# Two load queues shared out anew, a split last output tile, and a new table of due times in an attention and MLP kernel

## The chip, the cores and the metric

The kernel runs on one core of a Trainium2 chip. The metric is device time in microseconds (us) of one execution. A profile gives, beside the time, the span from the first to the last instruction of the program and what each engine did in it: PE (TensorE, matmuls), PEld (its weight loads), DVE (VectorE), ACT (ScalarE), POOL (GpSimd) and SP (SyncE, which here only issues DMAs).

## The reference

A linear attention over 8 batches and 8 heads of 576 positions of 64 features, and an MLP (512 to 2048 to 512, ELU between) over the 4608 tokens that come out of it.

```python
def phi(x):
    proj = np.einsum('bhsd,md->bhsm', x, omega)
    h = proj - np.sum(x * x, axis=-1, keepdims=True) / 2.0
    return np.exp(h - np.max(h, axis=-1, keepdims=True)) / np.sqrt(m)
q_p, k_p = phi(q * scale), phi(k * scale)          # m = 128, scale = 64 ** -0.25
kv = np.einsum('bhsm,bhsd->bhmd', k_p, v)
z = np.sum(k_p, axis=2)
num = np.einsum('bhsm,bhmd->bhsd', q_p, kv)
den = np.einsum('bhsm,bhm->bhs', q_p, z)[..., None] + 1e-06
x = (num / den).transpose(0, 2, 1, 3).reshape(4608, 512)
h = x @ w_in
g = np.where(h > 0.0, h, np.exp(np.minimum(h, 0.0)) - 1.0)
out = g @ w_out
```

w_in and w_out come as 64-bit floats.

## The kernel before, in words

The 64 heads are worked on as 32 pairs (two heads of 64 features fill 128 partitions), and the tokens as 9 blocks of 512. For each pair the keys are loaded (`xk`), squared, projected on the features (`ppk`, PE), their row minima taken (`mnk`, DVE) and exponentials made (`hk`, ACT, nine instructions of 128 columns); with the values `v` they give `pkv` (PE) and from it `kvf` and `z`. The queries go the same way (`xq`, `ppq`, `mnq`, `hq`); `pz` (PE) spreads `z`, DVE sums the denominators with it, `pt` (PE) turns the normalised queries, ACT copies them (`qh`), and `pn` (PE) makes the pair's attention output, which ACT and DVE write as a rounded part `xh` and a rest `xl`. Pairs 0 to 7 take this way with 32-bit matmuls (lines 551, 656, 844, 901); pairs 8 to 31 first split their inputs into two parts (`tk`, `tq`, line 419) and use line 601.

Layer 1 of the MLP makes, for a block and one of 16 slices of 128 hidden features, `ph` out of 12 matmuls of 512 columns (lines 1049 to 1051); ACT and DVE make the ELU out of it (`e`), which is split in `g`; layer 2 adds 12 matmuls to four accumulators `acc` (line 1094). The first two blocks go through the first eight slices, then through the others; in these first passes the weights are made out of 64-bit words (`raw_w`, `u_w`, `w1c`, `w2h`, `w2l`, lines 977 to 1010, five DVE instructions and an ACT one or two for each) and layer 1's are stored (`w1s`) and later loaded again into one of two buffers `w1c` (line 1030).

The order of all this is not the order of the code. Each step is an entry with an engine (or several that could do it), an expected duration, a due time and its buffers; a planner (`Plan.order`) plays them through before anything is built, starts on each free engine the ready entry that is due first, and the instructions are written out in the order found. Each engine then takes its own in that order and waits for the others by semaphores. The due times come from constants at the top (`MLP0`, `SEG`, `DUE_K`, `OFF1`, ...), `ALT` says how much an engine other than the first is held back for a kind of step, `STICK` how long PE keeps to a kind of matmul, `DMA_LAT` what a load is expected to take. An entry with `port=True` on DVE is not planned beside one on POOL, and POOL's next gets a wait for it.

At the start, pair 0's keys come in three pieces (positions 0 to 255 and 256 to 511 of both heads and the last 64) from SP, its queries in two from ACT's queue. At the end, each of the last block's four output tiles `o` of 128 tokens is copied by ACT and stored by SP.

Of the kernel before, what the change touches and what calls it, by code (L numbers as in the profile page):

```python
# [19 lines left out]
P = 128  # L20
# [23 lines left out]
NNAT = dict(k=8, q=8)  # L44


MLP0 = 32.36
SEG = [6.77, 5.04, 5.8, 7.72]
STEP = 6.67
STEP_ATT = 6.98  # L50

LAG = 3.0


PAIR0 = 12.06
DUE_LOAD, DUE_K, DUE_KV, DUE_Q = 63.96, 29.35, 20.2, 25.97
LOAD2, K2, KV2, Q2 = -116.39, 43.14, 31.66, 29.71
TAIL = 12.1
TAIL2 = 7.09
HEAD = 12.38  # L60


CONV1 = 9.62
CONV_STEP = -0.88
CONV2 = -8.25

EARLY = 12.91
CONV3 = 54.99


CROSS = False
# [1 line left out]
SPLIT = (0, 8, 16)  # L73
NHALF = 2

DUE_Z = 16.24


TURNED = 8
EARLIER = 10.63  # L80
QB = 32
NQB = P // QB
NTURN = 4
# [31 lines left out]
class Plan:  # L115
# [13 lines left out]
    SHARED = ("DVE", "POOL")  # L129

    FREE = dict(PE=1100.0, ACT=730.0, DVE=1600.0, POOL=1300.0, SP=700.0)
    DMA_LAT, DMA_RATE = 1500.0, 360.0

    def __init__(self):
        self.tasks, self.writer, self.readers, self.lands, self.behind = [], {}, {}, {}, {}
# [181 lines left out]


YIELD = 2e6
STICK = 1.25  # L320
SWITCH = 90.0
ENGINES = dict(DVE=mybir.EngineType.DVE, POOL=mybir.EngineType.Pool)


OFFP = [2.21, -0.6, 8.06, 9.4, -0.61, 1.49, 6.23, 2.21, 1.88, 6.13, -0.21, -0.78]
OFF1 = [6.25, -6.74, 0.99, -6.97, 4.74, 10.22, -12.88, -2.8, 6.03, 3.53, 4.6, 7.5, -11.77, 3.17, 9.25, 6.43]
OFF2 = [-6.65, 6.52, -4.52, -15.46, -12.1, -12.39, -1.42, -19.38, 26.89, 12.78, 21.89, 7.05, -2.21, 4.79, 12.27, -9.31]
DUE_V = 19.0


ALT = {'out': 46, 'conv_hi': 56, 'conv_sub': 10, 'g_lo0': -34, 'sq0': 5, 'sq1': -9, 'sq2': 1, 'norm0': 17, 'norm1': 112, 'norm2': 95, 'y_hi0': 95, 'y_hi1': 29, 'y_lo0': 40, 'y_lo1': 10, 'turn0': 73, 'turn1': 48, 'x_hi0': 36, 'x_hi1': 35, 'kv0': -6, 'kv1': 17, 'g_hi0': 65, 'g_hi1': 19, 'g_hi2': 19, 'g_lo1': -48, 'g_lo2': 34}


def other(kind, *engs):
# [3 lines left out]
def mm(n, m=1):  # L338

    return m * (n / 2.4 + 13.3)  # L340
# [15 lines left out]
def performer_elu_kernel(  # L356
# [110 lines left out]
    def load_pair(i, due):  # L467
        s = st.setdefault(i, {})

        def dma(dst, src, nbytes, *writes, early=False):  # L470
            nonlocal due
            if early:
                op("ACT", 600, -900 + due, lambda: nc.scalar.dma_start(dst(), src), (), writes, nbytes)
            else:
                op("SP", 590, due, lambda: nc.sync.dma_start(dst(), src), (), writes, nbytes)
            due += 0.01

        for nm, nat, mixed in (("k", k, kx), ("q", q, qx)):
# [21 lines left out]
    def project(i, nm, due):  # L500
# [15 lines left out]
        if native(i, nm):  # L516
# [25 lines left out]
            for g in range(3):  # L542
# [10 lines left out]
                def view(p=p):  # L553
                    return p().rearrange("p (j x) -> p j x", j=4)

                op("PE", 872 if g < 2 else 218, d, mms, [*([(x, g, 2)] if apart else [(x, a, 2) for a in range(2)]), "of"], (p,), full=1)
# [34 lines left out]
        for c in range(5):  # L591
# [11 lines left out]
            def view(p=p):  # L603
                return p().rearrange("p (a x) -> p a x", a=2)

            op("PE", mm(256, n) + 20, d, mms, [(y, a, z) for a in range(2) for z in "hl"] + ["oh", "om"], (p, (h, "slot", c)))
            def rest(c=c, n=n, p2=p2, view=view):
                for a in range(n):
                    j = 2 * c + a
# [339 lines left out]
    def from_f64(src, hi, lo, nm, due, key):  # L949
# [22 lines left out]
        def tail():  # L972
# [63 lines left out]
    def layer1(F, due):  # L1036
# [15 lines left out]

        for c in range(NC):
            reads = [(z, k) for k in ring(blk) if k[1] == c for z in ("xh", "xl")]
            op("PE", 688, due + 0.5 * c, lambda c=c: mms(c), [*reads, (w, "h"), (w, "l")], (p,))
# [23 lines left out]
    def layer2(F, due):  # L1079
# [19 lines left out]
            runs = [((tt,), (0, 1, 2)) for tt in range(NTT)]  # L1099
        else:  # L1100
            runs = [((2 * h, 2 * h + 1), (0, 1)) for h in range(2)] + [((2 * h, 2 * h + 1), (2,)) for h in range(2)]
        for e, (tts, which) in enumerate(runs):
            d = due + 0.65 * e
            op(
                "PE", 230 * len(tts) * len(which), d, lambda tts=tts, which=which: mms(tts, which),
                [*((g, passes[n][0]) for n in which), *(("w2", f, passes[n][2]) for n in which)], [now[tt] for tt in tts],
            )
            if not last:
# [147 lines left out]
```

## Time and profile before

| | us |
|---|---|
| median of 3 runs (lowest to highest) | 996.37 (995.45 to 998.47) |
| the profiled execution: its own time | 996.64 |
| the profiled execution: span | 994.8 |
| busy in the span: PE, ACT, DVE, POOL | 985.8, 654.4, 570.3, 475.8 |

The profiled execution is one like the others: 0.27 us above the median. A matmul's end is modelled in the profile, so a PE that shows as busy may hold short stalls; its starts are as recorded. Idle time of an engine other than the one that bounds the kernel costs nothing by itself.

### The profile page before, as it was taken

The numbers are of one execution on the slowest core, as the hardware profiler recorded it, in microseconds if no ns is written. First come the engines' busy times: TensorE is split into PE (matmuls) and PEld (weight loads), VectorE is DVE, ScalarE is ACT, GpSimd is POOL, SyncE is SP. The second block draws the span as 40 slices with busy tenths as digits, with TensorE's granted clock in tenths as the row PEclk, the third lists the DMA queues.
The fourth block names the chain that finished last, engine by engine and source line by source line (L and its number), as shares of the span: only waits on it lengthen the run. The fifth ranks groups of instructions, "written<-read, shape, count | busy, mean of one in ns | idle before, by whom it ended". The sixth has DMA issues, their size and how long they took to land.

```text
span 994.8 us, 17293 instructions
## 1 busy us (share of the span) xinstructions
PE 985.8 (99%) x5232; PEld 807.1 (81%) x5232; DVE 570.3 (57%) x2283; ACT 654.4 (66%) x1730; POOL 475.8 (48%) x438
## 2 busy tenths in 40 slices
PE   9999999999999999999999999999999999999998
PEld 9887788887788787887788778878788778888886
DVE  7999999679666555555555545555555421212121
ACT  7997657998877768776777578776877322223222
POOL 4555202576356656664657556665665322222222
PEclk9999999999999999999999999999999999999999
DMA  8666785468685555655575646555563333324231
GB/s 223 180 200 232 241 281 193 164 226 308 201 280 183 192 187 176 220 170 163 156 236 178 203 158 229 182 197 186 173 210 111 122 119 129 106 85 148 85 106 63
DMA packets 66716, 179.12 MB, mean 180 GB/s; under 512 B 9472, under 2 KB 22208, under 8 KB 66624
## 3 DMA queue, kind: packets, MB, share of 16 engines
q1 hardware_dynamic: 66256, 177.70, 54.5%
q8 instruction: 42, 0.69, 0.3%
q14 instruction: 50, 0.41, 0.1%
q10 hardware_dynamic: 368, 0.33, 0.1%
HBM read 143.92 MB, written 34.08 MB: 179 GB/s over the span
## 4 chain that ended last, share of the span: by engine, by line
PE 89%; DVE 5%; ACT 4%; DMA 1%; issue 1%; SPq 0%; ACTq 0%
PE acc L1094 37%; PE ph L1049 13%; PE ph L1051 12%; PE ph L1050 12%; PE ppk L601 2%; PE ppq L601 2%; PE pn L737 2%; PE ppk L551 1%; PE ppq L551 1%; DVE u_w L1000 1%; PE pkv L656 1%; DVE junk L821 1%; DMA w1c<-w1s 1%; PE pz L800 1%; ACT p2k L610 1%
## 5 line engine op out<-in xcount | busy, mean ns | idle before, releaser
L1094 PE MATMUL acc<-w2h,g 128*128 128x512 f32 x1152 | 392.2, 393 | 0.0
L419 POOL TENSOR_TENSOR g<-e,g 128x512 fp32r<-128x512 f32 x128 | 166.4, 1300 | 275.1 <-DVE g L416 200.4
L1094 PEld LDWEIGHTS acc<-w2h,g 128*128 128x128 f32 x1152 | 214.1, 188 | 40.9 <-issue 0.2
L1049 PE MATMUL ph<-xh,w1c 128*128 128x512 f32 x576 | 229.1, 398 | 0.6 <-DMA w1c<-w1s 0.4
L1058 ACT ACTIVATE e<-ph 128x512 f32<-128x512 f32 x144 | 85.6, 595 | 217.3 <-PE ph L1051 215.6
L1094 PE MATMUL acc<-w2l,g 128*128 128x512 f32 x576 | 227.7, 395 | 0.0
L1051 PE MATMUL ph<-xh,w1c 128*128 128x512 f32 x576 | 226.3, 393 | 0.0
L1050 PE MATMUL ph<-xl,w1c 128*128 128x512 f32 x576 | 225.9, 392 | 0.0
L416 DVE CAST g<-e 128x512 fp32r<-128x512 f32 x128 | 58.8, 460 | 188.6 <-PE acc L1094 183.2
L1062 DVE SCALAR_TENSOR_TENSOR e<-e,ph 128x512 f32<-128x512 f32 x144 | 98.7, 685 | 56.2 <-ACT e L1059 52.3
L1049 PEld LDWEIGHTS ph<-xh,w1c 128*128 128x128 f32 x576 | 108.3, 188 | 26.4 <-PE pn L901 1.5
L1051 PEld LDWEIGHTS ph<-xh,w1c 128*128 128x128 f32 x576 | 108.3, 188 | 24.3
L1094 PEld LDWEIGHTS acc<-w2l,g 128*128 128x128 f32 x576 | 108.4, 188 | 21.9 <-issue 0.9
L1050 PEld LDWEIGHTS ph<-xl,w1c 128*128 128x128 f32 x576 | 108.4, 188 | 19.7
L419 POOL TENSOR_TENSOR hq<-hq,den 128x512 f32<-128x512 f32 (+1 forms) x96 | 79.2, 838 | 62.6 <-DVE den L830 39.4
L419 POOL TENSOR_TENSOR tk<-xk,tk 64x576 fp32r<-64x576 f32 x48 | 70.4, 1467 | 78.7 <-ACT tk L414 64.8
L419 POOL TENSOR_TENSOR tq<-xq,tq 64x576 fp32r<-64x576 f32 x48 | 69.0, 1437 | 58.4 <-ACT tq L414 29.8
L1059 ACT ACTIVATE e<-e 128x512 f32<-128x512 f32 x144 | 91.8, 638 | 1.9
L619 DVE CUSTOM_DVE_ANT_0 hq<-ppq,p2q 128x128 f32<-128x128 f32 x216 | 53.8, 287 | 55.4 <-ACT p2q L610 48.1
L610 ACT ACTIVATE p2k<-ppk,sqk 128x128 f32<-128x128 f32 x216 | 66.4, 370 | 24.1 <-PE ppk L601 16.7
L610 ACT ACTIVATE p2q<-ppq,sqq 128x128 f32<-128x128 f32 x216 | 67.6, 379 | 21.0 <-PE ppq L601 19.9
L821 DVE CUSTOM_DVE_ANT_0 junk<-hq,pz 128x128 f32<-128x128 f32 (+1 forms) x320 | 73.9, 281 | 8.1 <-PE pz L800 7.3
(172 smaller groups left out, 1340.9 us busy)
## 6 DMA issues: line engine op xcount, KB each, us to landing
w1c<-w1s SPq DMA_DIRECT2D x128, 512.0 KB, 3.5
raw_w<-in_w_dram SPq DMA_DIRECT2D x32, 512.0 KB, 4.3
xk<-in_kx_dram SPq DMA_DIRECT2D x24, 576.0 KB, 4.5
xq<-in_qx_dram SPq DMA_DIRECT2D x24, 576.0 KB, 4.9
turned<-tb SPq DMA_DIRECT2D x24, 576.0 KB, 3.4
qh<-turned SPq DMA_DIRECT2D x96, 144.0 KB, 4.9
v<-in_v_dram SPq DMA_DIRECT2D x32, 325.0 KB, 4.3
out_dram<-o SPq DMA_DIRECT2D x36, 256.0 KB, 3.6
```

Source lines behind the costliest of these rows:

```text
L416: nc.vector.tensor_copy(dst, src)
L419: (nc.vector if e == "DVE" else nc.gpsimd).tensor_tensor(*args)
L610: nc.scalar.activation(p2()[:, a], view()[:, a, M:], AF.Identity, bias=sq()[:, j:j + 1], scale=1.0)
L619: nc.vector.tensor_tensor_reduce(out=h()[:, j, :], in0=view()[:, a, 0:M], in1=p2()[:, a, :], scale=1.0, scalar=HIGHEST, op0=ALU.add, op1=A ...
L821: nc.vector.tensor_tensor_reduce(out=junk()[r], in0=h()[r, j, :], in1=pz()[r, a * P:(a + 1) * P], scale=1.0, scalar=EPS, op0=ALU.mult, op1 ...
L1049: nc.tensor.matmul(ph(), wh, xh[:, c, o:o + TB], start=(c == 0), stop=False)
L1050: nc.tensor.matmul(ph(), wh, xl[:, c, o:o + TB], start=False, stop=False)
L1051: nc.tensor.matmul(ph(), wl, xh[:, c, o:o + TB], start=False, stop=(c == NC - 1))
L1058: op("ACT", act(TB, True), due, lambda: nc.scalar.activation(e(), ph(), AF.Relu, scale=-1.0), (p,), (e,))
L1059: op("ACT", act(TB), due + 0.2, lambda: nc.scalar.activation(e(), e(), AF.Exp, scale=-1.0), (e,), (e,))
L1062: lambda: nc.vector.scalar_tensor_tensor(e(), e(), -1.0, ph(), ALU.add, ALU.max), (p, e), (e,),
L1094: nc.tensor.matmul(now[tt](), g()[:, a, ts], w(), start=(first and n == 0), stop=(last and n == 2))
```

## The change

1. **Pair 0's loads.** Keys piece 1 and 2 and the queries' last piece go over SP's queue; the keys' last piece and the queries' big piece over ACT's.
2. **The last output tile.** The last matmul of 512 columns becomes two of 256; the first half of the tile is copied by ACT and stored by SP, the second copied by DVE and stored from ACT's queue.
3. **The table.** All due times, offsets and `ALT` values are new, as are a few expected durations; one more of the five DVE instructions of the weights' conversion (line 1000) is marked `port=True`.

```diff
-MLP0 = 32.36
+MLP0 = 39.956
...
-ALT = {'out': 46, ... 'sq2': 1, ... 'y_lo0': 40, 'y_lo1': 10, ...}
+ALT = {'out': 86, ... 'sq2': 49, ... 'y_lo0': 46, 'y_lo1': 0, ...}
...
-                    dma(dst, nat[i][:, :, s0:s0 + n], 2 * P * max(n, 2 * D) * 4, (t, key), early=i == 0 and nm == "q")
+                    dma(dst, nat[i][:, :, s0:s0 + n], 3 * P * max(n, 2 * D) * 2, (t, key), early=i == 0 and (key == 1) == (nm == "k"))
...
-            "DVE", dve(512), due - 5,
+            "DVE", 645, due - 5,
...
-            (u, (raw, 0)), (u,),
+            (u, (raw, 0)), (u,), port=True,
...
+            op("PE", 460, d, most, reads, (a,))
+            for k in range(2):
+                c = slice(k * DM // 2, (k + 1) * DM // 2)
...
+                op("PE", 117, d + 0.1 * k, half, [*reads, a], ((a, k),))
+                op(
+                    *(("ACT", act(DM // 2, True)), ("DVE", dve(DM // 2)))[k], d + 0.3 * k,
+                    lambda c=c, k=k: copy(("ACT", "DVE")[k], o()[:, c], a()[:, c]), ((a, k),), ((o, k),),
+                )
+                q = (nc.sync, nc.scalar)[k]
+                op(
+                    ("SP", "ACT")[k], 590, d + 1, lambda c=c, q=q: q.dma_start(out[r:r + P, c], o()[:, c]), ((o, k),), (),
+                    P * DM * 2,
+                )
```

`early` sends a load over ACT's queue; `key` is 0, 3 and 1 for the keys' three pieces and 0 and 1 for the queries' two.

**ACT's first instructions** (`xk_96` are pair 0's keys, `xq` its queries), before:

```order
L422 DMA of<-in_omT_dram 64x128
L473 DMA xq_109<-in_q_dram 64x2x512
L473 DMA xq_109<-in_q_dram 64x2x64
L1159 ACT_TABLE_LOAD
L530 ACTIVATE xk_96<-xk_96 64x2x256 x2
```

and now:

```order
L422 DMA of<-in_omT_dram 64x128
L473 DMA xk_96<-in_k_dram 64x2x64
L473 DMA xq_110<-in_q_dram 64x2x512
L1191 ACT_TABLE_LOAD
L530 ACTIVATE xk_96<-xk_96 64x2x256 x2
```

The queries' big piece goes out second instead of first, behind the keys' small one.

**ACT before the last exponential of pair 7's keys** (`hk_1124`, with `hq_1193` the same pair's queries and `tk`, `u_w`, `w1c` work for later steps), before:

```order
L414 COPY z_1191<-pkv_1114 128x2
L511 ACTIVATE hq_1193<-ppq_0_1130,mnq_1171 128x128 x4
L414 COPY qh_1137<-pt_2_1162 128x2x64
L414 CAST tk_1116<-xk_1024 64x576
L414 CAST w2h<-u_w_1_1073 128x512
L982 ACTIVATE u_w_4_1219<-raw_w_4_1154 128x512
L414 CAST w1c_1233<-u_w_6_1169 128x512
L511 ACTIVATE hk_1124<-ppk_2_1157,mnk_1107 128x128
```

and now (`hk_1203` are pair 7's keys; `qh_1250` is pair 6's, `e_1259` and `e_1197` belong to layer 1):

```order
L1059 ACTIVATE e_1197<-e_1197 128x512
L414 CAST w2h<-u_w_4_1059 128x512
L982 ACTIVATE u_w_6_1234<-raw_w_6_1122 128x512
L414 CAST tk_1242<-xk_873 64x576
L414 COPY qh_1250<-pt_0_1236 128x2x256
L1058 ACTIVATE e_1259<-ph_1208 128x512
L414 COPY qh_1250<-pt_1_1244 128x2x256
L1059 ACTIVATE e_1259<-e_1259 128x512
L511 ACTIVATE hk_1203<-ppk_1_1183,mnk_1189 128x128 x4
L511 ACTIVATE hk_1203<-ppk_2_1195,mnk_1189 128x128
```

More of pair 6's copies and of layer 1 stands ahead of pair 7's keys. Counted from the start of the queue to that instruction, ACT now has 7 more squares of queries (line 530; 10 instead of 3), 1 more of keys and 1 fewer of the later pairs' (line 570), 2 more copies `qh` of 512 columns, 2 more instructions on `e`, 1 more on `u_w`, 2 more casts `xh`, 4 fewer exponentials `hq` and 1 fewer cast `tk`. On PE, the first matmul that needs it (`pkv` of pair 7) has 4 fewer matmuls of layer 2, 9 fewer projections of queries and 9 more turning matmuls `pt` ahead of it.

**The last instructions of DVE and ACT**, with the semaphores that each waits for, now (`o_end` is the last tile; before, DVE had nothing there and ACT copied all 512 columns):

```order
L416 CAST g_11043<-e_11012 128x512 [waits DVE_49,PE_49,Pool_49]
L416 COPY o_end<-acc_0_3_10616 128x256 [waits Activation_49]
...
L414 COPY o_0_2_11070<-acc_0_2_10611 128x512 [waits PE_49,Pool_49]
L414 COPY o_end<-acc_0_3_10616 128x256 [waits PE_49,Pool_49]
L1127 DMA out_dram<-o_end 128x256 [waits DMAHW7_49,DVE_49]
```

DVE's half waits for ACT, whose own last copy is the one just before: the two halves stand one behind the other. Elsewhere, 77 of the 96 subtractions that make the second part of `tk` and `tq` moved from POOL to DVE, 16 of the casts of `g` from DVE to ACT, and six of the conversion's subtractions from DVE to POOL.

## Rows read from the trace of the kernel before

**Rows 1.** The page: busy time of the engines, and the granted clock in 40 slices.

```profile
PE 985.8 (99%) x5232; PEld 807.1 (81%) x5232; DVE 570.3 (57%) x2283; ACT 654.4 (66%) x1730; POOL 475.8 (48%) x438
...
PEclk9999999999999999999999999999999999999999
```

**Rows 2.** Waits of PE, whole span: who waited for whom, us, times, longest.

```profile
PE pz L796 <- ACT z L414: 1.3, 2, 1.0
...
PE pt L844 <- POOL hq L419: 0.9, 1, 0.9
PE ppk L551 <- ACT xk L530: 0.8, 1, 0.8
PE ph L1049 <- DMA w1c<-w1s: 0.4, 1, 0.4
PE ppk L601 <- ACT e L1059: 0.4, 1, 0.4
PE pkt L767 <- DVE mnq L619: 0.3, 1, 0.3
```

**Rows 3.** Stretches: length, then busy us of PE, PEld, DVE, ACT, POOL.

```profile
50.00:60.00 10.00, 10.00 (x63) 8.18 (x61) 9.99 (x38) 9.35 (x24) 5.19 (x5) 1.00 0.71 188
...
300.00:400.00 100.00, 100.00 (x516) 81.26 (x515) 58.01 (x284) 75.45 (x210) 60.71 (x57) 1.00 0.55 183
```

**Rows 4.** ACT alone from 0 to 81.74 us: length, busy; and its longest wait.

```profile
0.00:81.74 81.74, 73.42 (x219) 1.00 0.72 206
...
ACT hk L511 <- DVE mnk L559: 1.6, 2, 1.3
```

**Rows 5.** ACT's groups from 0 to 81.7 us: count, busy us, mean ns.

```profile
L511 ACT ACTIVATE hq<-ppq,mnq 128x128 f32<-128x128 f32 x68 | 20.0, 425 | 1.0 <-DVE mnq L559 1.0
L414 ACT COPY qh<-pt 128x512 f32<-128x512 f32 x12 | 7.4, 629 | 0.1
...
L414 ACT CAST xh<-pn 128x320 fp32r<-128x320 f32 x5 | 2.4, 478 | 0.0
...
L530 ACT ACTIVATE xq<-xq 64x576 f32<-64x576 f32 x3 | 2.0, 671 | 0.0
```

**Rows 6.** Timeline: start us, duration, engine, operation.

```profile
7.78 2.18 PE L551 MATMUL ppq<-of,xq 128*128 128x128 f32 x18
9.79 2.19 PE L551 MATMUL ppk<-of,xk 128*128 128x128 f32 x16
...
33.22 0.66 PE L844 MATMUL pt<-ident,hq 128*128 128x128 f32 x4
...
81.38 0.36 ACT L511 ACTIVATE hk<-ppk,mnk 128x128 f32<-128x128 f32 x1
...
85.48 0.39 PE L1094 MATMUL acc<-w2h,g 128*128 128x512 f32 x1
85.71 0.38 PE L651 MATMUL pkv<-v,hk 128*128 128x130 f32 x2
```

**Rows 7.** ACT's timeline at the start, and the DMAs of 2 to 6.5 us.

```profile
2.63 1.28 ACT L1159 ACT_TABLE_LOAD   x1 [2.63 <-issue]
...
5.88 0.63 ACT L530 ACTIVATE xk<-xk 64x512 f32<-64x512 f32 x1 [1.31 <-DMA xk<-in_k_dram]
...
DMA packets 1100, 0.96 MB, mean 214 GB/s; under 512 B 502, under 2 KB 822, under 8 KB 1100
```

**Rows 8.** Tile w1c, 96 to 135 us: its loads' time to landing.

```profile
DMA to landing us min/median/max: 3.0/4.0/6.2
```

**Rows 9.** The end: chain of work, DMA issues, a stretch; and copies of 256 columns.

```profile
991.37 0.58 ACT o L414
...
out_dram<-o SPq DMA_DIRECT2D x4, 256.0 KB, 2.0
...
990.50:993.35 2.85, 0.78 (x4) 0.31 (x2) 0.00 (x0) 1.26 (x3) 0.00 (x0) 1.00 0.92 343
...
82.64 0.72 ACT L414 CAST xh<-pn 128x256 fp32r<-128x256 f32 x2
```

More of the change, by code (lines that the diff above doesn't have):

```diff
@@ L44 @@
 NNAT = dict(k=8, q=8)
-MLP0 = 32.36
[L48 to L68, printed above, removed]
+MLP0 = 39.956
+SEG = [7.145, 5.059, 4.482, 9.812]
+STEP = 7.176
+STEP_ATT = 5.835
+LAG = 3.416
+PAIR0 = 12.847
+DUE_LOAD, DUE_K, DUE_KV, DUE_Q = 85.201, 38.49, 22.721, 19.9
+LOAD2, K2, KV2, Q2 = -32.31, 41.125, 31.418, 28.26
+TAIL = 17.575
+TAIL2 = -0.655
+HEAD = 23.823
+CONV1 = 15.95
+CONV_STEP = -1.049
+CONV2 = 3.454
+EARLY = 36.698
+CONV3 = 46.707
 CROSS = False
@@ L74 @@
 NHALF = 2
-DUE_Z = 16.24
+DUE_Z = 16.259
 TURNED = 8
-EARLIER = 10.63
+EARLIER = 13.794
 QB = 32
@@ L131 @@
     FREE = dict(PE=1100.0, ACT=730.0, DVE=1600.0, POOL=1300.0, SP=700.0)
-    DMA_LAT, DMA_RATE = 1500.0, 360.0
+    DMA_LAT, DMA_RATE = 1150.0, 360.0
     def __init__(self):
@@ L319 @@
 YIELD = 2e6
-STICK = 1.25
+STICK = 0.547
 SWITCH = 90.0
 ENGINES = dict(DVE=mybir.EngineType.DVE, POOL=mybir.EngineType.Pool)
[L325 to L331, printed above, removed]
+OFFP = [11.172, 11.247, 4.065, 8.746, 4.391, -4.123, -2.26, 14.007, 6.951, 6.668, -11.72, -6.174]
+OFF1 = [14.028, -3.158, -8.949, 0.591, 14.583, -9.49, -5.445, -9.428, 9.919, 7.941, 3.735, 8.176, 0.002, -1.956, 7.793, 12.064]
+OFF2 = [-6.728, -2.661, -8.129, -17.655, -18.863, 12.135, -2.051, -5.672, 2.608, 18.256, 28.172, 3.642, -8.266, -19.818, -24.304, 6.197]
+DUE_V = 45.529
+ALT = {'out': 86, 'conv_hi': 50, 'conv_sub': 0, 'g_lo0': -87, 'sq0': 11, 'sq1': -17, 'sq2': 49, 'norm0': 28, 'norm1': 115, 'norm2': 36, 'y_hi0': 62, 'y_hi1': 67, 'y_lo0': 46, 'y_lo1': 0, 'turn0': 86, 'turn1': 43, 'x_hi0': 16, 'x_hi1': 29, 'kv0': -10, 'kv1': 31, 'g_hi0': 76, 'g_hi1': -2, 'g_hi2': 38, 'g_lo1': -11, 'g_lo2': 27}
 def other(kind, *engs):
@@ L554, in view @@
                     return p().rearrange("p (j x) -> p j x", j=4)
-                op("PE", 872 if g < 2 else 218, d, mms, [*([(x, g, 2)] if apart else [(x, a, 2) for a in range(2)]), "of"], (p,), full=1)
+                op("PE", 893 if g < 2 else 223, d, mms, [*([(x, g, 2)] if apart else [(x, a, 2) for a in range(2)]), "of"], (p,), full=1)
                 op(
@@ L604, in view @@
                 return p().rearrange("p (a x) -> p a x", a=2)
-            op("PE", mm(256, n) + 20, d, mms, [(y, a, z) for a in range(2) for z in "hl"] + ["oh", "om"], (p, (h, "slot", c)))
+            op("PE", 247 if n == 2 else 128, d, mms, [(y, a, z) for a in range(2) for z in "hl"] + ["oh", "om"], (p, (h, "slot", c)))
             def rest(c=c, n=n, p2=p2, view=view):
@@ L1054, in layer1 @@
             reads = [(z, k) for k in ring(blk) if k[1] == c for z in ("xh", "xl")]
-            op("PE", 688, due + 0.5 * c, lambda c=c: mms(c), [*reads, (w, "h"), (w, "l")], (p,))
+            op("PE", 687, due + 0.5 * c, lambda c=c: mms(c), [*reads, (w, "h"), (w, "l")], (p,))
         due += 2
@@ L1101, in layer2, with tail, most, half @@
             runs = [((2 * h, 2 * h + 1), (0, 1)) for h in range(2)] + [((2 * h, 2 * h + 1), (2,)) for h in range(2)]
+        def tail(d):
+            a, r, ts = now[NTT - 1], NTOK - P, slice((NTT - 1) * P, NTT * P)
+            reads = [(g, 0), (g, 1), ("w2", f, "h"), ("w2", f, "l"), a]
+            o = Buf(sb, [P, DM], F32, "u", "o_end", 6)
+            def most():
+                for n, (e, w, _) in enumerate(passes[:2]):
+                    nc.tensor.matmul(a(), g()[:, e, ts], w(), start=False, stop=(n == 1))
+            op("PE", 460, d, most, reads, (a,))
+            for k in range(2):
+                c = slice(k * DM // 2, (k + 1) * DM // 2)
+                def half(c=c):
+                    nc.tensor.matmul(
+                        a()[:, c], g()[:, 1, ts], w2h[:, f, c], start=False, stop=True, skip_group_check=True
+                    )
[8 more added lines that the diff above has]
+                    P * DM * 2,
+                )
         for e, (tts, which) in enumerate(runs):
             d = due + 0.65 * e
+            if last and blk == NBLK - 1 and tts[0] == NTT - 1:
+                tail(d)
+                continue
             op(
-                "PE", 230 * len(tts) * len(which), d, lambda tts=tts, which=which: mms(tts, which),
+                "PE", 229 * len(tts) * len(which), d, lambda tts=tts, which=which: mms(tts, which),
                 [*((g, passes[n][0]) for n in which), *(("w2", f, passes[n][2]) for n in which)], [now[tt] for tt in tts],
```

## The prediction

> **What bounds the kernel now.** [...] So the time is PE's work plus the little time in which PE has nothing to do: 9.0 us of the span. The waits of PE show where: seven waits make 4.1 us of it [rows 2]; the rest is the head and the end of the program. The change leaves PE's matmuls as they are but for one that is halved, so it can move the time in three ways only: PE waits at other places than before, the start or the end gets shorter, or the transitions between kinds of matmul cost more. That caps the gain: even a PE that never waited would save about 4 us, 0.4%. A loss has no such cap.
>
> Next, the stretches say where waits can arise. From 300 to 400 us PE is busy for all of 100 us, with DVE at 58, ACT at 75 and POOL at 61: there everything that feeds PE has room. From 50 to 60 us PE, DVE and ACT are all full, 10.0, 9.99 and 9.35 of 10 us [rows 3]. The early phase, with the first eight pairs and the weights' conversion, is therefore where the new order decides, and I look there at what PE waits for and who makes it.
>
> **The change: ACT ahead of pair 7's keys.** PE takes its instructions in order; the first matmul `pkv` of pair 7 needs the last exponential of that pair's keys. Before, that exponential ended at 81.74 us and PE came to the matmul at 85.71 [rows 6]: 4.0 us to spare. Both ends move.
>
> ACT's side, from the counts in the order: 7 more squares at 0.67 (2.0 us busy for 3), 2 more on `e`, 1 on `u_w` and 1 on keys of about that length, while one cast `tk` and one longer square fall away; that is 9 at 0.67, 6.0. To that come 2 copies `qh` at 0.62 and 2 casts `xh` at 0.48, 2.2, less 4 exponentials at 0.29, 1.2. Sum 7.0 us [rows 5]. These are busy times; ACT's instructions overlap at their ends (the exponentials' mean is 425 ns against 294 busy for each), about 0.08 each over nine more instructions, so I take 6.2. ACT was busy for 73.42 of the 81.74 us before and idle for 8.32, of which 2.63 lie before its first instruction [rows 4, 7]: 5.7 us of idle time could take in part of the new work. If none is filled, the exponential ends at 87.9; if all, at 82.2. I take a middle. The wait of 1.31 for the second piece of pair 0's keys shrinks to 0.8 (below); the other 4.4, of which 1.6 is a wait for minima from a DVE that is full too, is half filled. That leaves 3.0, and the end at 81.74 + 6.2 - 5.7 + 3.0 = 85.2.
>
> PE's side: 4 fewer matmuls of layer 2 at 0.23 (the start distance of 85.48 and 85.71), 0.9; 9 fewer projections, which took from 7.78 to 9.79, 2.0; 9 more turns, four of which took 0.66, so 1.0 to 1.5, 1.0 taken since a matmul's end lies over the next [rows 6]. PE comes there 1.9 us earlier, at 83.8. So PE now waits 85.2 - 83.8 = **+1.4 us** where it did not wait; between no wait (and up to 1.5 gained, below) and +4.1.
>
> **The waits that go.** The longest wait, 1.0 us for `z` of pair 7 [rows 2], stands behind this one. In the new order ACT's `z` copy comes seven instructions after the exponential, while PE has about 9.5 us of matmuls between: it goes, **-1.0**. PE's 0.4 for a load of layer-1 weights was for slice 8 in block 1; its load now stands 10.5 us of PE work ahead of its use (46 matmuls of 512 columns at 0.23) instead of 5.5: **-0.4**. In its place, slice 10 has 4.6 us instead of 6.0 from the last use of its buffer to its own first; such loads took 3.0, 4.0 and 6.2 (least, median, most) [rows 8], so up to +1.6, and at the median nothing; I take **+0.2**. Two late waits, 0.4 for ACT and 0.3 for DVE [rows 2], may stay or go. Layer 2 runs further behind layer 1 (22.5 us of PE work between them in the middle of the 144 steps, before 12.4), which speaks for going. Half: **-0.35**.
>
> **The start.** The second piece of the keys held ACT up for 1.31 us and, through it, PE for 0.8 [rows 2, 7]. Before, the queries' 256 KB went out on ACT's queue beside it; now 32 KB go first. At the 214 GB/s of that stretch [rows 7] the 224 KB of difference are 1.05 us: the wait falls to 0.3 at best and stays at 1.31 at worst; I take the middle, 0.8. It is part of ACT's idle time above and not counted twice. [...]
>
> **The end.** The last copy took 0.58 us from 991.37 [rows 9]. The new order shows that DVE's half waits for ACT's. A half takes 0.36 (two casts of 256 columns in 0.72), so the second is done after 0.36 + 0.1 + 0.36 = 0.8, 0.25 later than now. Its transfer is half as long: the four tiles, 1.05 MB, moved at 343 GB/s [rows 9], so 128 KB less save 0.38. Sum -0.1 at best with the halves behind each other; the third tile's transfer is still under way then, and two issues instead of one cost something: **0**, from -0.3 to +0.3. [...]
>
> **Costed at nothing.** The 77 subtractions that go from POOL to DVE belong to pairs 8 to 31, at some 0.75 us each 58 us of DVE spread over stretches like that of 300 to 400, where DVE has 42 of 100 us free [rows 3]; without that cover each would delay PE by its length. The wait of POOL for line 1000 hides behind the same room. PE changes from 32-bit matmuls to the others 45 times instead of 46: nothing either way.
>
> **Sum**, against the profiled execution's 996.64: +1.4 - 1.0 - 0.4 + 0.2 - 0.35 + 0 = -0.15, 996.5. That execution was 0.27 above the median of the runs shown, so 996.2 for the median: no change. 0.3%, 3.0 us, is about what a measurement of this kernel can tell.
>
> **Rivals.**
> - *ACT keeps its idle time* (chance 0.22). ACT waited mostly for DVE, which is as full as before [rows 3, 4]; if those waits move along instead of being filled, the exponential ends at 87.9 and PE waits 4.1. With the two waits gone and the later ones kept: +4.1 - 1.0 - 0.4 + 0.2 = +2.9, 999.3 on the median's scale, and 1000.9 with the load's 1.6 on top: slower, or at the edge of it. It decides from the point where the exponential ends later than 86.8. Against it: an ACT with more work in its queue has something to do while it would have waited.
> - *ACT fills all of it* (0.12). The exponential ends at 82.2; PE's earlier waits of 0.9, 0.8 and 0.3 [rows 2] go too, so PE gains 1.5 there. -1.5 - 1.0 - 0.4 - 0.7 - 0.3 = -3.9, 992.5: faster. Against it: all three causes have to vanish in a phase where three engines are full.
> - *A new wait elsewhere* (0.08), such as slice 10's load at 6.2 or DVE's share in the full phase; one of 1.6 on top of the sum gives 997.8, and two make it slower.
> - The forecast, PE waiting 0 to 3 us for pair 7's keys and two old waits gone: 0.58.
>
> Of the forecast nearly all lies within 0.3%; of the first rival half is slower; of the second nearly all is faster. Together: faster 0.14, same 0.66, slower 0.20. The range goes from 992.8 to 1000.0; the forecast's own is 994.5 to 998.0.
>
> **What would show it.** The waits of PE should have a new entry at `pkv` (line 651) of pair 7 or just ahead of it, for ACT's `hk`, of about 1.4 us; `pz` waiting for `z` should be gone, and so should `ph` for slice 8's load near 115 us. ACT's first squares should wait about 0.8 for the keys. At the end, DVE's copy of 256 columns should begin after ACT's ended, and the time from the last matmul's start to the end of the span should stay within 0.3 us. The prediction is wrong if PE's waits before 100 us sum to over 7 us or under 1.5, or if PE shows waits after 250 us of more than 1 us together.

## The result and the profile after

The change made the kernel slower: 1003.31 us median against 996.77 for the kernel before, run on the same chip (22 runs of each), a ratio of 1.0059 with a 95% interval of 1.0047 to 1.0072. The prediction was 996.2, from 992.8 to 1000.0. One of the 22 runs of the changed kernel took 4300.5 us, in a slow state; it is in the median alone, which is 1002.83 without it, and neither in the ratio nor in what follows. The runs of the changed kernel also lie further apart: 999.2 to 1006.9, where nine with a mean granted clock of 1.000 (the share of full speed) have a median of 1002.0 and twelve with 0.996 to 0.999 one of 1004.9. So runs without a loss of clock are still 5.2 us slower than before, and the two groups lie 2.9 us apart in the median: the clock goes with the smaller part of the loss. The profiled execution is one of the upper ones, 1006.64 us with a span of 1004.9, 10.1 more than before.

The page first, its busy times:

```profile
span 1004.9 us, 17188 instructions
...
PE 990.7 (99%) x5233; PEld 810.3 (81%) x5233; DVE 617.5 (61%) x2339; ACT 672.5 (67%) x1754; POOL 359.7 (36%) x359
```

PE has the same matmuls as before, but for the one halved, and is busy for 4.9 us longer [rows 1]: a first sign of a lower clock, 0.996 in the mean of that execution, which the page's 40 digits don't show. DVE has 47 us more and POOL 116 less, as the order said. The waits of PE (who waited for whom, us, times, longest) say where PE stood:

```profile
PE pkv L651 <- ACT hq L511: 2.1, 1, 2.1
PE ph L1049 <- DVE e L1062: 1.3, 3, 0.7
PE ph L1049 <- DMA w1c<-w1s: 1.2, 1, 1.2
...
PE pz L800 <- ACT zr L711: 0.9, 1, 0.9
PE ppk L601 <- DVE mnk L619: 0.7, 1, 0.7
```

Of the entries of before [rows 2], `pz` for `z` and `pt` for POOL are gone, as is slice 8's load. The five shown are new or longer, 6.2 us together, and new ones of 0.6 us and less stand behind them. The longest stands at 22.82 us at `pkv` of pair 2, not of pair 7, and what came last there is not ACT's `hq`, which the row names and `pkv` does not read, but the load of pair 2's `v`: it was issued at 13.75 and took 8.9 us to land, to 22.7, while PE stood from 20.74 to 22.82. Three executions of variants of the changed kernel show it by name, `pkv <- DMA v<-in_v_dram`, 1.0, 1.4 and 1.8 us. SP's timeline tells why it was late (start, length of the issues, count):

```profile
9.21 1.54 SPq L977 DMA_DIRECT2D raw_w<-in_w_dram  x3
10.85 1.29 SPq L475 DMA_DIRECT2D xq<-in_q_dram  x2
13.75 0.33 SPq L475 DMA_DIRECT2D v<-in_v_dram  x1
14.26 1.19 SPq L475 DMA_DIRECT2D xk<-in_k_dram  x2
```

Three slices of weights, 512 KB each, stand ahead of pair 2's queries and values. The issues of 8 to 26 us, KB each and median us to landing, after and then before:

```profile
raw_w<-in_w_dram SPq DMA_DIRECT2D x3, 512.0 KB, 6.6
v<-in_v_dram SPq DMA_DIRECT2D x3, 325.0 KB, 5.8
...
xq<-in_q_dram SPq DMA_DIRECT2D x1, 256.0 KB, 9.0
```

```profile
raw_w<-in_w_dram SPq DMA_DIRECT2D x3, 512.0 KB, 5.0
v<-in_v_dram SPq DMA_DIRECT2D x3, 325.0 KB, 3.4
...
xq<-in_q_dram SPq DMA_DIRECT2D x3, 256.0 KB, 5.3
```

These medians mix several pairs. Pair 2's own loads changed more: its two of queries took 9.0 and 10.0 us instead of 5.0 and 4.6, its `v` 8.9 instead of 3.3. Before, those three slices were spread over these 18 us, one ahead of pair 2's queries and the others behind the next pairs' loads. After that wait PE is slow for a while. Stretches: length, busy us of PE, PEld, DVE, ACT, POOL, then the granted clock, the DMAs' share and GB/s:

```profile
22.00:24.00 2.00, 1.18 (x11) 1.21 (x12) 0.58 (x2) 1.14 (x4) 1.76 (x2) 1.00 0.46 129
24.00:26.00 2.00, 2.00 (x14) 2.00 (x13) 1.86 (x6) 0.68 (x1) 0.32 (x1) 0.59 0.07 23
26.00:28.00 2.00, 2.00 (x13) 2.00 (x12) 1.38 (x13) 1.22 (x3) 1.42 (x3) 0.56 0.52 142
```

The granted clock falls to 0.50 of full speed, from 24.4 to 27.8 us. What that costs, estimated from the clocks of these two rows, in which PE is busy throughout, is 2 x (1 - 0.59) + 2 x (1 - 0.56) = 1.7 us. The fall stands behind the one long gap of this phase, the 2.1 us.

It happens once more, at the other end of a longer chain. ACT's timeline, and PE's beside it:

```profile
531.15 0.69 ACT L570 ACTIVATE xk<-xk 128x576 f32<-128x576 f32 x1 [2.75 <-DMA xk<-in_kx_dram]
...
536.99 0.39 ACT L711 CAST zr<-zs 128x256 fp32r<-128x256 f32 x1
```

```profile
537.44 0.84 PE L800 MATMUL pz<-zr,ones 128*128 128x256 f32 x2 [0.89 <-ACT zr L711]
```

```profile
538.00:540.00 2.00, 1.59 (x6) 1.21 (x7) 2.00 (x13) 0.94 (x4) 0.95 (x1) 0.94 0.72 267
540.00:543.00 3.00, 3.00 (x9) 2.41 (x9) 2.11 (x22) 0.48 (x2) 2.42 (x3) 0.50 0.01 3
543.00:545.00 2.00, 2.00 (x10) 1.61 (x9) 1.25 (x6) 1.81 (x7) 0.40 (x1) 0.95 0.01 4
```

The square of pair 24's keys stands at the head of ACT's queue 2.75 us before the keys have landed, and none of the instructions behind it starts in that time: they run in the order of the queue. With thirteen between them comes `zr`, for which PE then waits 0.89, and two shorter gaps later (0.07 and 0.41 us) the clock falls again: PE's matmuls of 512 columns start 0.42 us apart at 0.50 and 0.23 at 1.00. By the clocks of the rows that is another 1.7 us, estimated as above (0.06 x 2 + 0.50 x 3 + 0.05 x 2). ACT's waits for the loads of late pairs, after and before:

```profile
ACT xq L570 <- DMA xq<-in_qx_dram: 8.6, 4, 2.3
ACT xk L570 <- DMA xk<-in_kx_dram: 4.3, 3, 2.7
```

```profile
ACT xk L570 <- DMA xk<-in_kx_dram: 2.7, 2, 2.1
...
ACT xq L570 <- DMA xq<-in_qx_dram: 2.2, 2, 1.9
```

12.9 us in seven places against 4.9 in four. The last of the new waits of PE, 1.24 us at 308 us, is a load of layer-1 weights that was issued at 301.21 behind a pair's queries, two `v` and four turned blocks, and took 8.8 us; such loads took 3.0 to 6.2 in the early stretch of before [rows 8].

The profile's 10.1 us, then: 5.2 are idle time of PE (1004.9 - 990.7 against 994.8 - 985.8), of which 2.6 lie in the first 100 us (busy 93.14 against 95.78, by the stretches below) and the rest behind, where the waits 0.7 + 1.2 + 0.9 + 0.6 make 3.4 and the small ones of before made 1.3. The other 4.9 are longer busy time. The two stretches at the lower clock make 3.4 of that, by the two estimates above; the last 1.5 no row explains. The prediction's third way, dearer transitions between kinds of matmul, is not ruled out for it, but no run shows what a transition costs.

```profile
0.00:100.00 100.00, 93.14 (x663) 81.16 (x664) 85.52 (x302) 87.74 (x248) 41.04 (x46) 0.98 0.67 198
```

```profile
0.00:100.00 100.00, 95.78 (x692) 83.62 (x693) 91.94 (x330) 85.87 (x246) 52.75 (x54) 1.00 0.71 210
```

### The profile page after: what moved, and what is told of

It is laid out like the page before. It is cut to its first block, busy times and chain, and to the rows that moved or that the text cites. A ratio compares the mean times of both kernels' runs of the same rounds, so it can differ in the third digit from the quotient of the medians.

```text
span 1004.9 us, 17188 instructions
## 1 busy us (share of the span) xinstructions
PE 990.7 (99%) x5233; PEld 810.3 (81%) x5233; DVE 617.5 (61%) x2339; ACT 672.5 (67%) x1754; POOL 359.7 (36%) x359
## 4 chain that ended last, share of the span: by engine, by line
PE 85%; ACT 7%; DMA 5%; DVE 2%; issue 1%; SPq 0%; ACTq 0%; POOL 0%; DVEq 0%; POOLq 0%
PE acc L1094 37%; PE ph L1049 12%; PE ph L1051 12%; PE ph L1050 12%; PE ppk L601 2%; PE ppq L601 2%; PE pn L737 2%; DMA xk<-in_kx_dram 2%; ACT hq L511 1%; ACT hk L511 1%; DMA out_dram<-o 1%; DMA w1c<-w1s 1%; DMA xq<-in_q_dram 1%; ACT xq L530 1%; DMA xk<-in_k_dram 1%
## 5 line engine op out<-in xcount | busy, mean ns | idle before, releaser
L1094 PE MATMUL acc<-w2h,g 128*128 128x512 f32 x1150 | 367.2, 392 | 0.0
L416 DVE CAST g<-e 128x512 fp32r<-128x512 f32 x112 | 49.4, 441 | 38.7 <-PE acc L1094 38.4
L511 ACT ACTIVATE hq<-hq,mnq 128x128 f32<-128x128 f32 x216 | 68.7, 398 | 1.9 <-DVE mnq L619 1.5
L511 ACT ACTIVATE hk<-hk,mnk 128x128 f32<-128x128 f32 x216 | 68.6, 396 | 0.8 <-DVE mnk L619 0.2
```

What stands on the lines that cost most here:

```text
L511: nc.scalar.activation(h()[:, j, :], src(j), AF.Exp, bias=mn()[:, j:j + 1], scale=-1.0)
L1094: nc.tensor.matmul(now[tt](), g()[:, a, ts], w(), start=(first and n == 0), stop=(last and n == 2))
```

## The experiments

Three theories stood against each other. *Loads*: loads are issued in bunches, or read too early, and PE pays through `pkv`, `ph` and, by way of ACT, `pz`. *ACT*: its added work ahead of pair 7's keys, the prediction's main term. *Moves*: the steps given from POOL to DVE, line 1000's port wait, the halved tile. Where an experiment changes the order alone, the planner's list is made as before and entries are then moved in it, so that every other row on every engine stays as it was; `put` does that, by entry numbers:

```diff
+    def put(self, order, tasks, behind):
+        moved = [r for n in tasks for r in order if r[0] == n]
+        left = [r for r in order if r[0] not in tasks]
+        at = [n for n, _ in left].index(behind) + 1
+        return left[:at] + moved + left[at:]
```

Line numbers of an experiment's profile are higher by what was put in; the tiles' names are the same. Each was timed beside the kernel before, whose median was 996.8 to 997.1 throughout.

### The parts of the change alone

The first edit alone, in the kernel before (the loads' places in the order as in the changed kernel):

```diff
+            queue = nc.scalar if other else nc.sync
...
+                    dma(..., early=i == 0 and nm == "q", other=i == 0 and (key == 1) == (nm == "k"))
```

> The kernel before with the change's first edit alone: the last columns of pair 0's keys are issued on ACT ahead of its queries, the last columns of its queries on SP; the order of everything else is that of before. All theories: ACT's wait for the second piece of the keys falls from 1.31 us to 0.3 to 0.8, and the time is 0.5 us shorter, at most 1.0, at least 0.

996.87, ratio 0.9999 (0.9987 to 1.0010): nothing. ACT's wait for the second piece was 1.10 in that execution; 0.32 stands in the changed kernel's own profile and 1.0 to 1.6 in those of its variants. PE's 0.8 for the keys is gone here, but one of 0.7 for `hk` stands at 31 us, where the kernel before's profile has none.

The second edit alone is the change's own `tail` in the kernel before.

> The kernel before with the change's second edit alone, the last output tile in two halves; the order of everything else is that of before. Loads and ACT theories: DVE's half waits for ACT's, so the end is within 0.3 us of before's. Moves theory: if the halves are part of the loss, 0.5 us or more slower.

997.41, ratio 1.0004 (0.9992 to 1.0015): nothing. The changed kernel's own end shows why:

```profile
1001.29 0.37 ACT L414 COPY o_end<-acc 128x256 f32<-128x256 f32 x1
1001.69 0.36 SPq L1127 DMA_DIRECT2D out_dram<-o_end  x1
1001.70 0.42 DVE L416 COPY o_end<-acc 128x256 f32<-128x256 f32 x1 [5.48 <-ACT o_end L414]
```

DVE's half begins when ACT's is done. Neither edit loses anything by itself, so what is left is the table.

### The early loads

The kernel before with its second and third slice load put where the change has them, ahead of pair 2's queries:

```diff
         order = self.order()
+        order = self.put(order, [223, 232], 240)
```

> The kernel before, with nothing moved but its second and third weight slice load, put ahead of pair 2's queries behind the first one, as the changed kernel has them. Loads theory: PE waits 1.5 to 2.5 us for pair 2's v at its pkv at 20 to 24 us, the clock falls to half for some 3 us after it, and the time rises by 3 to 5 us, to 1000 to 1002. ACT theory and moves theory: ACT's, DVE's and POOL's order is that of before, so 996.8 within 1 us.

1000.35, ratio 1.0027 (1.0014 to 1.0039): 3.3 us lost by two rows of SP's queue, with no other row on any engine changed. PE's wait came at the queries, not at `v`, and 1.97 of its 2.3 us in one piece:

```profile
PE ppq L558 <- POOL xq L426: 2.3, 2, 2.0
```

```profile
22.00:24.00 2.00, 1.47 (x5) 1.18 (x6) 0.00 (x0) 0.53 (x3) 1.92 (x3) 0.50 0.36 121
24.00:26.00 2.00, 2.00 (x11) 2.00 (x11) 0.96 (x3) 0.00 (x0) 1.74 (x3) 0.50 0.01 3
26.00:28.00 2.00, 2.00 (x12) 2.00 (x11) 0.69 (x2) 1.41 (x3) 1.10 (x1) 0.50 0.54 136
```

To price the clock by itself, the same kernel with eight matmuls that nothing reads, where PE waited:

```diff
                 def mms(g=g, p=p):
+                    if i == 2 and nm == "q" and g == 0:
+                        for _ in range(8):
+                            nc.tensor.matmul(p()[:, 0:P], ident, ident, start=True, stop=True)
```

> The kernel before with the two weight slice loads put early, as run already (1000.35), and eight matmuls of 128x128 that nothing reads put on PE ahead of pair 2's first projection of queries, where PE waited 1.97 us. If the stretch at half clock after that wait is a good part of the 3.3 us, the clock stays at full speed with PE kept busy and the time falls by 1 to 2 us, to 998.4 to 999.4. If the wait itself is all, nothing changes, or it gets up to 0.5 us longer.

998.46, ratio 1.0013 (1.0003 to 1.0022), 1.9 us better than without them, and in the profile the clock stays at 1.00, where it was 0.50:

```profile
22.00:24.00 2.00, 1.46 (x12) 1.12 (x10) 0.20 (x1) 0.49 (x2) 1.92 (x3) 1.00 0.52 130
24.00:26.00 2.00, 2.00 (x19) 2.00 (x20) 1.94 (x4) 1.30 (x3) 1.92 (x3) 1.00 0.28 44
```

So a good half of the 3.3 us was the clock. The runs without the extra matmuls say the same: three with a mean granted clock of 1.000 have a median of 997.9, the nine others one of 1000.7. The other way round, the changed kernel without its early bunch (and the two ACT steps that read those slices put later with them):

```diff
+        order = self.put(order, [232, 257], 174)
+        order = self.put(order, [233], 148)
+        order = self.put(order, [258], 106)
```

> The changed kernel, with nothing moved but two of its three early loads of weight slices (the second and the third) from ahead of pair 2's queries to behind pair 3's v in SP's queue, and the two ACT steps that read them some 12 us later. Loads theory (SP's queue in the first 25 us is what costs): the 2.1 us wait of PE at pair 2's pkv falls under 0.5 us, the stretch at half clock from 24.4 to 27.8 us goes with it, and the time falls by 3 to 5 us, to 998.5 to 1000.5. ACT theory (the work ahead of pair 7's keys is what costs): ACT has the same work ahead of pair 7's keys, so the time stays within 1 us of 1003.3. Moves theory (the steps given to other engines, the port wait and the halves at the end): within 1 us of 1003.3 too.

1002.14, ratio 1.0047 (1.0033 to 1.0061): 1.2 us better and not 3 to 5, and with intervals that overlap not clear of noise. The wait at `pkv` and the slow stretch are gone from the profile, as expected, but the wait for the slice load at 306 us was 2.0 us in that execution and others stayed. No stretch at the lower clock follows that wait, the granted clock is 1.00 from 300 to 400 us: here a wait of this length did not bring one. The start is not all, then, and the loads theory in its first form falls short. One number of the table put back, with a new plan, was a worse test:

```diff
-EARLY = 36.698
+EARLY = 12.91
```

> The changed kernel with one number put back, the bound on how far ahead of its due time a weight slice's load may be issued (12.91 us in place of 36.698), and its order planned anew: the three early slice loads then stand behind pair 3's keys in SP's queue, not ahead of pair 2's queries. Loads theory: PE's 2.1 us wait at pair 2's pkv goes with the half clock after it, 2 to 4 us faster than the changed kernel, 999.3 to 1001.3. ACT and moves theories: within 1 us of 1003.3. Since the order is planned anew, new waits of up to 2 us elsewhere can hide part of it.

1011.81, ratio 1.0144 (1.0129 to 1.0160). The slices' loads went behind pair 3's keys and the wait at `pkv` to 0.1, but all else was planned anew by due times that were made for the other number: PE waited 3.6 us for slice loads, 2.3 for ACT's `qh`, 1.5 for `mnk` and 1.5 for POOL. It says nothing on the theories but that such a number can't be taken back by itself.

### The start against the rest

Two splices of both orders, at 141 us of planned time:

```diff
-        order = self.order()
+        order = []
+        for row in ROWS.split():
...
```

> The changed kernel's instructions and both its edits, but issued in the order of the kernel before for the first 141 us (planned time) and in the changed order from there on; 17 steps of the conversion of one weight slice and of a layer-2 sum change sides at the seam. Start theory (what is lost is lost in the first 100 us): 997 to 998.5. Spread theory (half or more is lost in the layer stages, from 150 us on, by waits for loads and for ACT): 1000 or more. The two splices' losses against 997.0 should add up to the whole, 6.3 us, if the halves don't act on each other.

> The converse: the changed order for the first 141 us, that of the kernel before from there on. Start theory: 1001.5 to 1003.5, with PE's 2.1 us wait at pair 2's pkv as in the changed kernel. Spread theory: 1000 or less.

1008.86 (1.0105, 1.0084 to 1.0125) and 1004.38 (1.0074, 1.0053 to 1.0096): the two losses, 12.0 and 7.6 us, don't add up to 6.3, because the seam makes losses of its own. Of each, the wait that stands right behind the seam, at 152 and 155 us:

```profile
PE ppk L802 <- DVE e L1263: 1.8, 1, 1.8
```

```profile
PE acc L1297 <- DVE g L619: 2.3, 1, 2.3
```

The mean granted clock of each of the two executions was 0.998. The times decide nothing.

### The layer stages

Edits to the changed kernel, each at one of its places. The loads ahead of the slice load at 301 us put behind the next ones:

```diff
+        order = self.put(order, [1649, 1720], 1893)
+        order = self.put(order, [1565, 1566, 1567, 1568], 2041)
```

> The changed kernel with the loads of two pairs' v (behind the second next slice load) and of one pair's four turned blocks (behind the next keys) taken from ahead of the slice load issued at 301 us, which took 8.8 us to land; their readers come some 30 us later. Loads theory: PE's wait of 1.24 us at 308 us goes, with what follows it, and the time falls by 1.2 to 2 us. ACT and moves theories: nothing.

1002.73, ratio 1.0074 (1.0047 to 1.0100), seven runs from 999.7 to 1008.2: unclear. In the profile the wait for the load is gone, and `pz` waits for `zr` instead, at 317 and 426 us, some 6 us behind waits of ACT of 2.1 and 2.4 us for keys:

```profile
PE pz L808 <- ACT zr L719: 1.6, 2, 1.1
```

Two of ACT's conversion steps put later, for the ACT theory:

```diff
+        order = self.put(order, [272], 410)
+        order = self.put(order, [309], 601)
+        order = self.put(order, [273], 463)
```

> The changed kernel with two of ACT's weight conversion steps (the copy of slice 3's second weights, 0.52 us, and the first step of slice 5, 0.57 us) put from ahead of pair 6's and 7's work to behind the copies of pair 5's result, and the one DVE step that reads the first of them with it. ACT theory (ACT, full from 70 to 84 us, delays PE there): PE's waits of 0.28, 0.64 and 0.69 us between 75 and 83 us shrink by 1 us or more in all, and the time falls by 1 to 2 us. Loads theory: at most 0.5 us.

1002.37, ratio 1.0053 (1.0039 to 1.0067). The wait of 0.28 at 75 us is gone, that of 0.64 stayed and that of 0.69 grew to 1.39: the sum is larger than in the changed kernel, and the time is not clearly another. All three edits so far (the early bunch and these two) together:

> The changed kernel with three of these edits together: the two early slice loads behind pair 3's v, the two ACT steps put later, the loads ahead of the slice load at 301 us put later. If the losses add up: -1.2 (as measured for the first), -1.2 to -2 and 0 to -1.5, so 998.6 to 1001, and the waits that are left are one at ACT's zr step between 426 and 643 us and those of the first 75 us. If each wait removed is met by another, no better than 1002.1.

1001.74, ratio 1.0042 (1.0027 to 1.0057), between the two forecasts, with new waits in the profile: `pz` for `zr` in three places, 2.0 us, and 1.7 for DVE at 81 us. What comes back in each of these profiles is ACT at a load of keys or queries in the layer stages, mostly at the same places, every fourth pair. So I moved ACT's reading of the loads. First all of it:

```diff
+LATER = [([1280], 1282), ([1324], 1024), ([1325], 1164), ...]
...
+        for tasks, behind in LATER:
+            order = self.put(order, tasks, behind)
```

> The changed kernel with each square of a late pair's keys or queries (pairs 10 to 31, the ACT step that reads a load first) put some 2 us of ACT's rows later in ACT's queue, and its DVE sum behind it; their readers come some 30 us later. Slack theory (the changed order reads loads before they land, ACT stands at them, and its next steps reach PE late): ACT's waits for these loads, 12.9 us in the changed kernel against 4.9 before, fall to 5 or less, PE's waits at pz, at ph and at ppk after 150 us (4 us with their stretch at half clock) mostly go, and the time falls by 1.5 to 3 us. Start theory (all that matters happens in the first 100 us): within 0.5 us of 1003.3.

1007.10, ratio 1.0100 (1.0074 to 1.0126): slower. ACT's waits for these loads are almost gone, 1.7 us for keys with none listed for queries, and none of PE's waits is for `zr`'s ACT step, but DVE's rows now come late: `ppk`, `pz` and `ph` wait for `xl` and `sqq`, at 309, 352, 461, 569 and 679 us.

```profile
PE ph L1060 <- DVE sqq L584: 1.3, 1, 1.3
...
PE ppk L612 <- DVE xl L943: 0.9, 1, 0.9
PE pz L811 <- DVE xl L943: 0.9, 3, 0.3
```

The same with the early loads and the slice load put later:

> The same squares put later, and with them the two early slice loads behind pair 3's v and the loads ahead of the slice load at 301 us put later. Slack theory with loads theory: little is left but the waits of the first 90 us, some 3 us more than before's, so 998 to 1000. If waits are only exchanged for others: 1001 or more.

1003.94, ratio 1.0067 (1.0046 to 1.0088): better by 3.2 us, at the edge of the noise, with the waits for `xl` left. The converse, in the kernel before, is clear:

> The kernel before with the squares of pairs 10 to 31 put some 1.4 us of ACT's rows earlier, as the changed planner places them. Slack theory: ACT's waits for these loads grow from 4.9 us to 9 or more, PE gets waits after 200 us, and the time rises by 1 to 2 us. Otherwise 996.9 within 0.5 us.

1009.31, ratio 1.0113 (1.0084 to 1.0142), 12 us lost by moving these ACT rows alone. ACT's waits for the loads are 11.5 us instead of 4.9, and PE has a wait of a kind that the kernel before had not:

```profile
ACT xq L581 <- DMA xq<-in_qx_dram: 8.2, 6, 2.8
ACT xk L581 <- DMA xk<-in_kx_dram: 3.3, 2, 2.6
```

```profile
PE ph L1060 <- ACT kvf L425: 5.2, 4, 2.6
```

It stands at 351, 459, 571 and 681 us, once in four pairs, the longest 2.6 us, and the mean granted clock of that execution is 0.998. The size is larger than the 1 to 2 us expected, since the same place is hit in every round of four pairs; one more wait, 1.6 us for `xl`, stands at 254. That named the rows to try in the changed kernel: the four squares of keys that stand some 6 us ahead of `zr` in ACT's queue, put just behind it.

```diff
+        order = self.put(order, [2044], 1677)
+        order = self.put(order, [2045], 1900)
...
```

> The changed kernel with four ACT rows moved, the squares of the keys of pairs 16, 20, 24 and 28, each from some 6 us ahead of the zr step in ACT's queue to just behind it, and its DVE sum likewise. Slack theory, now by its place (ACT stands at these loads for 0.7 to 2.7 us, and the zr step behind them reaches PE's pz late): PE's wait at pz of 0.9 us at 536 us, and those of the runs since at 317, 426 and 643 us, are gone, with the stretch at half clock that can follow; 1 to 3 us faster than the changed kernel, 1000 to 1002.3. If the load waits of ACT are not what reaches PE: within 0.5 us of 1003.3.

1004.75, ratio 1.0069 (1.0043 to 1.0095), six runs from 1001.5 to 1008.2. The waits at `pz` are gone, all of them; the profile holds the wait for `v` (1.8 us, with the clock at 0.50 from 24 to 29 us behind it) and that at 310 us (1.2). By itself it shows no gain. With the other two places mended as well:

> The changed kernel with all load edits that aim at one wait each: the two early slice loads behind pair 3's v, the loads ahead of the slice load at 301 us put later, and the four squares behind zr. If these three places hold the loss: 998 to 1000, with no wait of PE over 0.5 us after 175 us, and an excess before 100 us of some 10.5 us against before's 7.5. If waits are only exchanged: 1001 or more.

999.85, ratio 1.0029 (1.0018 to 1.0040), twelve runs from 998.4 to 1002.6, eleven of them with a mean granted clock of 1.000. The interval lies below that of the change itself, 1.0047 to 1.0072: by the ratios, 1.0029 against 1.0059, these three places together hold half of the loss. How it is shared among them is not shown, since none of the three edits alone is clear of noise. PE's waits:

```profile
PE ph L1068 <- DVE e L1081: 1.5, 4, 0.7
...
PE pt L863 <- ACT hq L530: 0.6, 1, 0.6
PE ph L1068 <- ACT hk L530: 0.5, 1, 0.5
```

After 175 us none is over 0.5. In this profile PE's idle time is 1.1 us above that of before (997.6 - 987.5 against 994.8 - 985.8), all of it in the first 100 us, where PE is busy for 94.63 us against 95.78. Its busy time is 1.7 us above, at a mean granted clock of 1.000; the same matmuls took 985.8 to 987.0 in the profiles of the kernel before and of its two edits, so part of that is noise. The last run asked whether ACT makes what is left:

> The changed kernel with the three load edits that aim at one wait each (999.85 together) and the two ACT steps put later as well. What those three leave against before, 2.8 us, lies in the first 100 us. If ACT, full from 25 to 84 us, is what makes it: 1 us or more better, 998.9 or less. If ACT's waits there only change places: 999.3 to 1000.4.

1001.69, ratio 1.0046 (1.0032 to 1.0060), five runs: no gain. A wait of 1.7 us for DVE's `e` stands in its profile, as it did with the three edits together, where ACT's steps were put later too; 0.7 stood there without that.

### Holes of the kernel before

> The kernel before with two rows moved: POOL's first square of pair 7's queries from ahead of pair 4's scaling to behind it (PE waited 0.86 us for that at 60 us), and DVE's copy of pair 7's sums from behind a layer-1 step to ahead of it (PE waited 1.0 us for the z that hangs on it, at 88 us). If what stands in the chain is worth its wait: 0.8 and 0.6 us, 995.4 against 996.8. If a later wait takes what was given back, within 0.3 us of before.

```diff
+        order = self.put(order, [540], 404)
+        order = self.put(order, [538], 536)
```

997.77, ratio 1.0006 (0.9995 to 1.0017). In the profile the wait for POOL at 60 us is gone and the one for `z` is 0.35 instead of 1.0, but waits for ACT's `hk` came in their place: 0.96 at 31 us, where the kernel before had none, and 0.82 at `pz` at 83 us instead of 0.26.

```profile
PE ppq L559 <- ACT hk L519: 1.2, 2, 1.0
PE pz L804 <- ACT hk L519: 0.8, 1, 0.8
```

PE is busy for 94.84 of the first 100 us, less than the 95.78 of before. Two waits that the change also took away were so exchanged for others; what they are worth when nothing takes their place is not shown. No version that I found beats the kernel before.

## Why the prediction was wrong

**The failed step is the choice of the place.** "The early phase [...] is therefore where the new order decides", read from the stretches, was half right, but the sum then priced one queue in it, ACT's ahead of pair 7's keys, and one more at the start. On SP's queue it priced pair 0's loads, slice 8's and slice 10's and the last stores, and nothing between. That three slice loads now stood ahead of pair 2's queries and values was in the order, and the profile of before had the rate: at the 214 GB/s of the start [rows 7], the two additional 512 KB are, by estimate, 4.9 us of transfer in front of a `v` that PE wanted at 20.7 us (22.82 less its wait). Measured, pair 2's queries landed 4.0 us later after their issue (9.0 against 5.0) and its `v` 5.6 (8.9 against 3.3). In the kernel before this alone costs 3.3 us. It is one place of three; the others are a slice load at 301 us and ACT's squares ahead of `zr`, and together they hold half of the loss. Which step makes the other half is open.

**The term for pair 7's keys: +1.4, measured 0.** ACT's last exponential of pair 7 is the last of these five, and PE's `pkv` follows it:

```profile
88.64 1.37 ACT L511 ACTIVATE hk<-ppk,mnk 128x128 f32<-128x128 f32 x5
```

```profile
90.39 0.38 PE L651 MATMUL pkv<-v,hk 128*128 128x130 f32 x2
```

It ends at 90.01, and PE comes 0.4 later, without a wait. Both are later than forecast (85.2 and 83.8), and PE more. The loss at the start is not what closed the gap, for without the early bunch, where neither that wait nor the slow stretch is left, the two stand just as close, at 87.81 and 88.19:

```profile
86.41 1.40 ACT L520 ACTIVATE hk<-ppk,mnk 128x128 f32<-128x128 f32 x5
```

```profile
88.19 0.39 PE L660 MATMUL pkv<-v,hk 128*128 128x130 f32 x2
```

The prediction moved PE's end by its matmuls alone, as if PE could not lose time upstream of the place. How much of PE's delay ACT made there itself is not shown. Where I then looked for ACT's part, in waits of 0.28 to 0.69 between 75 and 83 us, putting ACT's steps later exchanged them for others.

**"Everything that feeds PE has room" from 300 to 400 us: wrong as a reason.** A busy share of 75% did not show that ACT, whose rows ran in the order of its queue, would stand at a load. ACT's waits for late pairs' loads went from 4.9 to 12.9 us over the layer stages, and PE's after 250 us sum to 2.7, over the 1 us that the prediction named as its own refutation.

**The clock was not in the sum at all.** A wait was priced at its length. Of the 3.3 us that a wait of 2 us cost in the kernel before, the eight idle matmuls gave back 1.9; in the profiled execution the clock accounts, by estimate, for 3.4 of 10.1 us. It is not the main part of the loss: the nine runs at a mean granted clock of 1.000 are still 5.2 us above the kernel before.

**What held, and what did not.** The waits for `z` of pair 7 and for slice 8's load went, as forecast, and slice 10's load brought none; but in the experiment on the holes other waits took the place of such ones, and the time did not fall. The halves stand one behind the other and the end is worth nothing. ACT's wait at the start did not hold: it is 0.32 in the changed kernel's own profile, but 1.0 to 1.6 in those of all its variants, against 1.31 before, so the forecast of 0.8 was too low; the edit alone is worth nothing.

**The rivals.** The right one was the smallest, "a new wait elsewhere", at 0.08: right in kind, and its price of 1.6 too low, since there were three such places and two brought a stretch at the lower clock. The range up to 1000.0 was too short by the prediction's own words: a loss was said to have no cap, and the first rival's price went to 1000.9. The remaining 2.8 us, of which the profile shows waits of 0.2 to 0.7 us in the first 85 us and some longer busy time, are not settled: ACT's steps there were tried and are not shown to be the cause, and the subtractions on DVE, behind the waits for `e`, were not tried apart.

## What to carry to other kernels

When an order is replanned, go through the queue of the engine that issues loads as closely as through those that compute: for each load, the bytes now ahead of it at the rate of that stretch (here 4.9 us by that estimate, 4.0 to 5.6 measured), against the time to its first reader. Then look at the first reader itself, and whether it stands in its engine's queue close to the time at which the load can land: here a square stood 2.75 us at a load, the thirteen rows and the `zr` behind it started only after it, PE waited 0.89 us for `zr`, and a stretch in which ACT was busy for 74 of 100 us, 500 to 600, was no cover. One number of a table of due times put back was no test here, since all else was planned anew; freeze the order and move single rows instead, and look for the waits that take the place of those removed.

## What the runs showed of the hardware

- The granted clock fell in mid-kernel. After a wait of PE of 2.1 us in the first 25 us it was at 0.50 from 24.4 to 27.8 us; in the kernel before, with waits up to 1.0 us, it was 1.00 in every stretch of 2 us up to 994 us. Where such a wait of 2.0 us was followed by 0.50 from 22 to 28 us, eight matmuls that nothing reads, put into it, left the clock at 1.00 and were worth 1.9 us.
- Such a wait did not bring the low clock each time: after one of 2.0 us at 306 us, in the changed kernel without its early bunch, the granted clock was 1.00 from 300 to 400 us.
- Here a load's time to landing went more by what stood in the queue ahead of it than by its own size: pair 2's 32 KB of queries took 10.0 us behind three slices and 256 KB and 4.6 behind one slice and 256 KB, when slices of 512 KB took 5.0 in the median of the same stretch before.
